# A fused attention and GLU block: where VectorE's code operations stand against background jobs at the end of a head group

## The chip, the cores and the metric

The kernel runs on one core of a Trainium2 chip. The metric is the device time of one execution in microseconds (us). An execution that was profiled gives, beside its time, the span from its first to its last instruction and the record of every instruction in it.

## The reference

```python
x = A_x                                             # (1, 2048, 512) bf16
h  = x + attention(layernorm(x), A_wqkv, A_wo)      # 32 heads of 16
h2 = h + glu(layernorm(h), B_w_gate, B_w_up, B_w_down)   # F = 1792

# attention: scores = q k^T * 16**-0.5; p = softmax(scores); o = p v; o @ wo
# glu:       (sigmoid(x @ w_gate) * (x @ w_up)) @ w_down
```

The bulk is the softmax: 32 heads x 2048 queries x 2048 keys is 134 million exponentials.

## The kernel before, in words

**Tiling.** The scores are computed transposed, 128 keys in the partitions and 512 queries in the free dimension, for one head: such a block is a *unit*. There are 2048 units. The heads come in groups: 32 *head groups* in the order of a list `gseq`, each of 64 units (16 key tiles by four row positions j). Six groups are four heads by 512 queries, the other 26 ("wide") eight heads by 256 queries, two heads to a unit. Three units make a *score tile* (`pss`, 128x1536 in PSUM, two buffers), so there are 683 score tiles, numbered through all groups.

**Who computes the exponentials.** For each score tile ScalarE runs `exp` over three units (a 128x1536 instruction) or over two (128x1024, line 1227), and in the second case VectorE does the third unit with integer arithmetic: a first operation `J` out of PSUM (line 1054) makes the bits of an approximate power of two, and when four units of J (sometimes fewer) are together in one tile, three further additions `code` (line 1074, 128x2048 for four units) make three more bit patterns of other rounding. J and the three codes are all multiplied with V and summed, so a unit on VectorE costs one J, three quarters of a code instruction, and four products on TensorE in place of one. The three code operations that wait to be issued are a `Chain` in the list `chains`.

**What follows.** TensorE multiplies each exponential with `Vaug` (V and a column for the sums) into one accumulator `acc` (line 1028, a single PSUM bank, one group at a time). When all products of a group are in, VectorE transposes `acc` into `xs` (line 970), divides (lines 932 and 934) and turns the result into `ot` (line 946). Only then may the products of the next group begin.

**Background work.** Everything else runs beside the exponentials, in small steps through one PSUM tile `pm` with a single buffer: projections of V, K and Q, and, block by block of 256 rows, the output projection with the residual (`wo_add`, lines 695 and 708), the layer norm (statistics at line 133, the Newton steps for the inverse root in lines 657 to 680, the scaling at line 720, the transposes on TensorE at line 151 and VectorE's copy out of `pm` at line 734), the gate and up products (line 160; `th`, the tanh on ScalarE at line 759, and `hT` on VectorE at line 743) and the down products (line 753 writes `ob`). The helper `quarters` at line 160 issues most of these matmuls. `fill` (line 505) issues a matmul whose result nobody reads, where TensorE would be little used.

**What sets the order.** The program is one straight line of instructions per engine. While it is built, a planner steps through three virtual clocks, `T["P"]`, `T["A"]` and `T["D"]` for TensorE, ScalarE and VectorE, with costs written in the code; the engine whose clock is earliest takes its next step (`pe_step` at line 1131, `act_step` at 1182, `dve_step` at 1241), and that step is issued. So the order of each engine's queue is fixed in the program, and on the chip each instruction waits only for what it needs. `act_step` takes a ready ScalarE job such as `th` before the next `exp` if the job's inputs are ready by the planner's clock no later than 100 ns after that `exp` could start (line 1188), and it also decides whether VectorE gets a unit of the tile, by the backlog of VectorE. `dve_step` takes, in this order: a ready background job that fits before the next J; the next J whose scores are done; a ready background job out of `dq` (line 1257); the next operation of the first chain (line 1263). `nxt["e"]` counts the score tiles whose `exp` has been issued, `lasts[group]` is the number of the last tile of a group, and `st["cur"]` the place in `gseq` of the group whose products TensorE is at.

Of the kernel before, what the change touches and what calls it, by code (L numbers as in the profile page):

```python
# [26 lines left out]
def kernel(  # L27
# [174 lines left out]
    class Task:  # L202
        def __init__(self, name, deps, opts, bank=0, frees=0):
            self.name, self.deps, self.opts, self.bank, self.frees = name, deps, opts, bank, frees
            self.end = None
            tasks[name] = self
# [221 lines left out]
    dq, aq, chains = [], [], []  # L428
# [8 lines left out]
    st = State(**{"n": 0, "open": False, "cur": 0, "pm": None, "mark": None, "acc": None, "mode": "b", "work": "b", "ot": 0})  # L437
# [7 lines left out]
        return aq[-1]  # L445

    class Chain:
        def __init__(self, ops, after):
            self.ops, self.after = deque(ops), after

        def left(self):
            return sum(o[0] for o in self.ops)
# [8 lines left out]
    def next_chain():  # L461
        return chains[0]

    def pop_chain():
        c = next_chain()
        T["D"] += c.cost()
        _, _, f = c.ops.popleft()
        c.after.append(object())
        prior["op"] = c.after[-1]
        f()  # L470
        if not c.ops:
            chains.remove(c)
# [161 lines left out]
    gseq = [(0, 0), (1, 0), (2, 0)]  # L634
# [221 lines left out]
    firsts, lasts = {}, {}  # L856
# [52 lines left out]
    NPT = 6  # L909
    PRESS = 3  # L910
    EASY = 400
    RATE, LATE, BACK, GEND, QMAX = 0.7, 700, 2500, 2000, 24

    ring = []
# [124 lines left out]
    NCODE = len(CODE_STEP)  # L1039
# [8 lines left out]
    def dexp_first(src, un):  # L1048
        if not half:
            half.append(dvx.tile([P, NJ, QC], U16, name="J", bufs=NJB))  # L1050
            first_codes.append([1])
        J, held = half[0], first_codes[-1]
        k = len(half) - 1
        first = nc.vector.tensor_scalar(out=J[:, k, :], in0=src, scalar1=128 * SC * LOG2E,  # L1054
                                        scalar2=float(CODE_BASE), op0=ALU.mult, op1=ALU.add)
        half.append(un)
        held[0] += 1
        avq.append(Unit(un.u, J[:, k, :].bitcast(BF16), un.n, T["D"] + 680, held))
        prior["op"] = J
        if k == NJ - 1:  # L1060
            dexp_rest()
        return first

    def dexp_rest():
        J, uns = half[0], half[1:]
        half.clear()
        k = len(uns)
        j = J[:, 0:k, :]
        mine = first_codes[-1]
        mine[0] += NCODE - 1  # L1070

        def code(i):
            c = dvx.tile([P, NJ, QC], U16, name="code", bufs=CB)[:, 0:k, :]
            nc.vector.tensor_scalar(out=c, in0=j, scalar1=CODE_STEP[i], scalar2=None, op0=ALU.add)  # L1074
            mine[0] -= 1
            held = [k]
            codes.append(held)
            avq.extend(Unit(un.u, c[:, m, :].bitcast(BF16), un.n, T["D"] + 85, held)
                       for m, un in enumerate(uns))
            for un in uns:  # L1080
                due[un.u[0], un.u[1], un.u[3]] -= i == NCODE - 1
        chains.append(Chain([(75 + 134 * k, 0, lambda i=i: code(i)) for i in range(NCODE)], [J]))

    def drop_read():
        for c in (codes, first_codes):
            while c and not c[0][0]:
                c.popleft()
# [41 lines left out]
    nxt = {"s": 0, "e": 0}  # L1129
# [52 lines left out]
    def act_step():  # L1182
# [15 lines left out]
        if half and not jq and left_in.get(half[-1].u[:2], 0) < CLOSE:  # L1198
            dexp_rest()
# [7 lines left out]
        if (len(tl) == GU and not 10 <= n < 20 and len(jq) < 2  # L1207
# [9 lines left out]
            if good:  # L1217
                pick = good[0]
            elif can and back <= EASY:
                pick = can[0]  # L1220
# [20 lines left out]
    def dve_step():  # L1241
        t = T["D"]
        job = next((j for j in dq if j.ready() is not None and j.ready() <= t), None)
        if job and jq and t - sc_end[jq[0][0]] < 400:
            dq.remove(job)
            job.place("D")
            return
        drop_read()
        if jq and sc_end[jq[0][0]] + LAT <= t + WAITJ and (half or len(first_codes) < NJB):
            n, pss, un, ex = jq.popleft()  # L1250
            first = dexp_first(pss, un)
            T["D"] = max(t, sc_end[n] + LAT) + 600
            ex_end[n] = max(un.end, T["D"])
            tc.declare_no_dep(first.ins, ex.ins, reason="other banks of the tile")
            readers[n] = (ex, first)
            return
        for job in dq:
            r = job.ready()
            if r is not None and r <= t + 60:
                dq.remove(job)  # L1260
                job.place("D")
                return
        if chains:
            pop_chain()
            return
        T["D"] = t + 40
# [21 lines left out]
    while nxt["e"] < N or jq:  # L1288
        e = nxt["e"]
        if e == N:  # L1290
            dve_step()
            continue
        steps[min("PAD", key=lambda k: T[k])]()
        if nxt["e"] > e:
            after_exp(e)
    if half:
        dexp_rest()
# [106 lines left out]
```

## Time and profile before

| | |
|---|---|
| time, median of 3 runs | 826.86 us (826.76 to 828.12) |
| profiled execution, its time | 826.86 us |
| profiled execution, its span | 825.1 us |
| ScalarE busy | 779.8 us (95%) |
| TensorE matmuls busy | 751.6 us (91%) |
| VectorE busy | 734.3 us (89%) |
| `exp` on ScalarE, line 1227 | 683 instructions, 727.8 us |
| `J` on VectorE, line 1054 | 478 instructions, 318.1 us |
| `code` on VectorE, line 1074 | 387 instructions, 237.4 us |
| `acc` products, line 1028 | 6337 instructions |
| `hT`, line 743, out of `pm` | 49 instructions, 33.3 us |
| `th`, line 759, out of `pm` | 49 instructions, 30.7 us |

How to read it: a row of the profile gives the line, the engine, the operation, output and inputs by the program's names, the form, and the count; then the time in which the engine was busy with these instructions, the mean length of one in ns, and the engine's idle time just before them, with what ended most of that idle time. Instructions of one engine can overlap a little, so the busy time may be below count times mean. What lies outside the span, 826.86 - 825.1 = 1.8 us, belongs to no instruction.

### The profile page before, as it was taken

Reading aid. Unit: us, or ns where it says so; the run is one execution under the profiler, and the core shown is the slowest. Engines: PE = TensorE matmul, PEld = TensorE weight load, DVE = VectorE, ACT = ScalarE, POOL = GpSimd, SP = SyncE. Lnnn points to the kernel's source line nnn. Section 1 sums busy time; section 2 is a strip of 40 time slices with the busy share of each in tenths; the row PEclk is TensorE's granted clock in tenths of the full one; section 3 lists DMA queues with packets and bytes.
Section 4 is the critical chain, followed back from the end, with each engine's and each line's share of the span. In section 5 each row is a group of like instructions: output and inputs, shape, how many; then the busy total and the mean of one; then the engine's idle time right before and its main releaser. Section 6 shows DMA issues by size and latency. Waiting matters only on the chain.

```text
span 825.1 us, 34604 instructions
## 1 busy us (share of the span) xinstructions
PE 751.6 (91%) x15255; PEld 364.5 (44%) x15259; DVE 734.3 (89%) x1415; ACT 779.8 (95%) x804; POOL 3.2 (0%) x8
## 2 busy tenths in 40 slices
PE   4889988887889999999999999999899999999988
PEld 2322223333335344555444444553455455455546
DVE  8849999997999999999989899889999889899972
ACT  6899999998999999999989999999999999989972
POOL 1000000000000000000000000000000000000000
PEclk9999999999999999999999999999999999999999
DMA  9700011015001121122022211220132022134110
GB/s 259 130 2 4 16 34 27 13 31 159 8 16 54 42 82 35 47 82 78 16 74 61 64 36 47 81 78 16 45 104 84 28 80 79 48 98 141 43 39 16
DMA packets 90717, 49.47 MB, mean 60 GB/s; under 512 B 20820, under 2 KB 90120, under 8 KB 90568
## 3 DMA queue, kind: packets, MB, share of 16 engines
q1 hardware_dynamic: 88936, 46.15, 21.1%
q8 instruction: 121, 1.98, 0.9%
q10 hardware_dynamic: 1632, 1.11, 0.4%
q14 instruction: 28, 0.23, 0.1%
HBM read 37.62 MB, written 2.10 MB: 48 GB/s over the span
## 4 chain that ended last, share of the span: by engine, by line
ACT 45%; PE 33%; issue 14%; DVE 7%; DMA 0%; ACTq 0%; DVEq 0%
ACT pt L1227 42%; PE pm L160 11%; PE pss L887 9%; PE acc L1028 9%; DVE J L1054 2%; ACT th L759 2%; PE gu L155 2%; DVE code L1074 1%; PE hp L1369 1%; DVE xs L970 1%; PE b L151 0%; DVE st L133 0%; DMA code<-in_A_x_dram 0%; DVE hT L743 0%; DVE xn L238 0%
## 5 line engine op out<-in xcount | busy, mean ns | idle before, releaser
L1227 ACT ACTIVATE pt<-pss 128x1024 bf16<-128x1024 f32 (+1 forms) x683 | 727.8, 1192 | 9.4 <-PE pss L887 6.6
L1054 DVE TENSOR_SCALAR J<-pss 128x512 uint16<-128x512 f32 x478 | 318.1, 681 | 24.5 <-PE pss L887 22.9
L887 PE MATMUL pss<-QT,KT 32*128 32x256 bf16 (+1 forms) x3712 | 269.5, 284 | 50.4 <-ACT pt L1227 39.6
L1074 DVE TENSOR_SCALAR code<-J 128x2048 uint16<-128x2048 uint16 (+3 forms) x387 | 237.4, 643 | 0.3
L1028 PE MATMUL acc<-pt,Vaug 128*17 128x256 bf16 (+1 forms) x2837 | 219.2, 286 | 2.0 <-ACT pt L1227 0.8
L887 PEld LDWEIGHTS <-KT 32*128 32x128 bf16 x3712 | 84.9, 92 | 251.3 <-ACT pt L1227 128.8
L1028 PE MATMUL acc<-code,Vaug 128*17 128x256 bf16 (+1 forms) x2625 | 186.4, 284 | 0.0
L1028 PEld LDWEIGHTS <-Vaug 128*17 128x17 bf16 x6337 | 139.7, 90 | 97.8 <-issue 82.2
L1028 PE MATMUL acc<-J,Vaug 128*17 128x256 bf16 (+1 forms) x875 | 137.2, 284 | 0.1
L160 PE MATMUL pm<-xnT,wgu 128*32 128x256 bf16 x3136 | 117.6, 275 | 1.6 <-DVE hT L743 0.8
L160 PEld LDWEIGHTS <-wgu 128*32 128x32 bf16 x3136 | 77.6, 96 | 27.2 <-issue 23.5
L160 PE MATMUL pm<-wd,hT 128*32 128x512 bf16 x784 | 56.1, 382 | 0.0
L743 DVE SCALAR_TENSOR_TENSOR hT<-th,pm 128x512 bf16<-128x512 f32 x49 | 33.3, 679 | 10.1 <-PE pm L160 8.8
L759 ACT ACTIVATE th<-pm 128x512 f32<-128x512 f32 x49 | 30.7, 626 | 8.3 <-PE pm L160 7.3
L970 DVE STREAM_TRANSPOSE xs<-acc 128x512 f32<-128x512 f32 x32 | 22.8, 712 | 11.5 <-PE acc L1028 11.3
L160 PEld LDWEIGHTS <-hT 128*32 128x32 bf16 x784 | 16.0, 95 | 19.6 <-issue 13.1
L160 PE MATMUL pm<-xnT,wq_sb 128*32 128x512 bf16 x256 | 20.5, 391 | 0.2 <-DVE kr L566 0.2
L160 PE MATMUL pm<-xnT,wk_sb 128*32 128x512 bf16 x256 | 19.7, 383 | 0.1
L151 PE MATMUL b<-ident_bf,xn 128*128 128x128 bf16 x64 | 6.5, 265 | 12.1 <-DVE xn L238 11.4
L160 PE MATMUL pm<-wo_sb,ot 128*32 128x512 bf16 x224 | 17.2, 382 | 0.1
L946 DVE STREAM_TRANSPOSE ot<-o 128x256 bf16<-128x256 bf16 x32 | 13.6, 433 | 0.1
L604 DVE TENSOR_SCALAR sh<-pm,kcol 8x512 bf16<-8x512 f32 x16 | 11.8, 735 | 1.9 <-PE pm L600 1.7
(126 smaller groups left out, 327.2 us busy)
## 6 DMA issues: line engine op xcount, KB each, us to landing
wgu<-in_B_w_gate_dram SPq DMA_DIRECT2D x49, 256.0 KB
wgu<-in_B_w_up_dram SPq DMA_DIRECT2D x49, 256.0 KB
KT<-ones SPq DMA_DIRECT2D x7, 512.0 KB
out_dram<-ob SPq DMA_DIRECT2D x16, 128.0 KB
QT<-qd SPq DMA_DIRECT2D x116, 16.0 KB
KT<-kd SPq DMA_DIRECT2D x28, 64.0 KB
wd<-in_B_w_down_dram SPq DMA_DIRECT2D x1, 1792.0 KB
xr<-in_A_x_dram SPq DMA_DIRECT2D x14, 128.0 KB
```

The source lines that it names most:

```text
L155: nc.tensor.matmul(ps, lhsT=lhsT, rhs=rhs, start=start, stop=stop)
L160: nc.tensor.matmul(ps[r, :], lhsT=lhsT[:, r], rhs=rhs, start=start, stop=stop, tile_position=(0, 32 * j), skip_group_check=True)
L604: nc.vector.tensor_scalar(out=sh[:], in0=ps2[0:8, :], scalar1=-0.505, scalar2=kcol[p][:, 0:1], op0=ALU.mult, op1=ALU.add)
L743: nc.vector.scalar_tensor_tensor(out=hT[:, 2 * k:2 * k + 2, :].rearrange("p f q -> p (f q)"), in0=th[:], scalar=1.0, in1=ps, op0=ALU.add, ...
L759: nc.scalar.activation(out=th[:], in_=ps, func=ACT.Tanh, scale=0.5)
L887: mm = nc.tensor.matmul(pss[:, ui, a * w:(a + 1) * w], lhsT=KT[hg[a]][32 * j:32 * j + 32, kt * P:(kt + 1) * P], rhs=(QT0[q] if g == 0 and ...
L946: nc.vector.transpose(out=ot[:], in_=o2[:, i * NB:(i + 1) * NB, :] .rearrange("p b r -> p (b r)"))
L970: j = st["acc"] = dve(630, lambda: nc.vector.transpose(out=xs[:].rearrange("p b r -> p (b r)"), in_=acc[:]), Mark(T["P"]))
L1028: nc.tensor.matmul(acc[32 * j:32 * j + VW, a * w:(a + 1) * w], lhsT=Vaug[:, kt, 4 * hg[a] + j, :], rhs=un.ap[:, a * w:(a + 1) * w], start= ...
L1054: first = nc.vector.tensor_scalar(out=J[:, k, :], in0=src, scalar1=128 * SC * LOG2E, scalar2=float(CODE_BASE), op0=ALU.mult, op1=ALU.add)
L1074: nc.vector.tensor_scalar(out=c, in0=j, scalar1=CODE_STEP[i], scalar2=None, op0=ALU.add)
L1227: ex = nc.scalar.activation(out=pt[:, lo:lo + wa, :], in_=pss[:, lo:lo + wa, :], func=ACT.Exp, scale=SC)
```

## The change

A chain now carries the group that its units belong to. In `dve_step`, behind the J and ahead of the background jobs, a new step is tried: if the first chain belongs to the group that TensorE's products are at, and the `exp` of that group's last score tile has been issued, the next code operation of that chain goes first. `HURRY` is 0: "has been issued" is meant exactly.

```diff
     class Chain:
-        def __init__(self, ops, after):
-            self.ops, self.after = deque(ops), after
+        def __init__(self, ops, after, group):
+            self.ops, self.after, self.group = deque(ops), after, group
...
+    HURRY = 0
...
-        chains.append(Chain([(75 + 134 * k, 0, lambda i=i: code(i)) for i in range(NCODE)], [J]))
+        chains.append(Chain([(75 + 134 * k, 0, lambda i=i: code(i)) for i in range(NCODE)], [J], uns[0].u[:2]))
...
             readers[n] = (ex, first)
             return
+        if chains and chains[0].group == gseq[st["cur"]] and lasts[chains[0].group] < nxt["e"] + HURRY:
+            pop_chain()
+            return
         for job in dq:
             r = job.ready()
             if r is not None and r <= t + 60:
```

Because the planner issues what its clocks bring next, an operation that changes place moves all later choices with it: which tiles give a unit to VectorE, where background steps of TensorE fall, and where `th` stands among the `exp`.

## The prediction, made before the changed kernel was run

> **What bounds the kernel now.** I read the page's first part, then the busy time of the stretch from the first to the last `exp`, then ScalarE's waits in that stretch. The columns of the second fence are the stretch, its length, and the busy time of TensorE, of its weight loads, of VectorE, ScalarE and GpSimd; then the granted clock and the DMA columns.
>
> ```profile
> PE 751.6 (91%) x15255; PEld 364.5 (44%) x15259; DVE 734.3 (89%) x1415; ACT 779.8 (95%) x804; POOL 3.2 (0%) x8
> ```
>
> ```profile
> 33.00:795.70 762.70, 707.41 (x14918) 337.24 (x14918) 695.85 (x1306) 746.36 (x732) 0.30 (x1) 1.00 0.19 54
> ```
>
> ```profile
> ACT th L759 <- PE pm L160: 7.3, 5, 3.0
> ACT pt L1227 <- PE pss L887: 6.6, 14, 1.9
> ACT pt L1227 <- PE acc L1028: 0.9, 1, 0.9
> ```
>
> In the stretch of 762.7 us ScalarE is busy for 746.36, idle for 16.3; TensorE has 55 us to spare and VectorE 67. So the stretch lasts as long as ScalarE's work plus its waits, and the last fence names 14.8 us of those. What the change is worth is what it does to these two sums.
>
> Where the 14.8 us lie I took from ScalarE's timeline: three of the waits, 1.49 us before 251.05, 2.99 before 418.27 and 2.40 before 733.05, together 6.9, are a `th` at the first gate product of a new block. Each lies within 2.5 us after a transpose of `acc` (249.3, 415.9, 731.8), so at a group's end; all waits so placed make 9.0. The last of the three, ScalarE, VectorE and TensorE in order of time:
>
> ```profile
> 729.62 1.03 ACT L1227 ACTIVATE pt<-pss 128x1024 bf16<-128x1024 f32 x1
> ...
> 729.92 0.41 DVE L734 COPY xnT<-pm 128x512 bf16<-128x512 bf16 x1
> 730.25 1.02 DVE L1074 TENSOR_SCALAR code<-J 128x1024 uint16<-128x1024 uint16 x2
> 730.71 0.40 PE L887 MATMUL pss<-QT,KT 32*128 32x256 bf16 x6 [0.52 <-DVE code L1074]
> ...
> 731.04 0.40 PE L151 MATMUL pm<-ident_bf,xnT 128*128 128x128 bf16 x4
> ...
> 731.47 0.43 DVE L734 COPY xnT<-pm 128x512 bf16<-128x512 bf16 x1 [0.20 <-PE pm L151]
> 731.81 0.71 DVE L970 STREAM_TRANSPOSE xs<-acc 128x512 f32<-128x512 f32 x1
> 731.95 1.06 PE L160 MATMUL pm<-xnT,wgu 128*32 128x256 bf16 x32 [0.20 <-DVE xnT L734]
> ...
> 733.05 0.60 ACT L759 ACTIVATE th<-pm 128x512 f32<-128x512 f32 x1 [2.40 <-PE pm L160]
> ```
>
> The reader is to see a string with nothing beside it: the `exp` ends at 730.65, releases a score bank, TensorE does scores, the last layer-norm transposes, VectorE copies them, TensorE does the gate product, and only then `th` runs. Scores for a next `exp` lay ready from about 731.1, but `th` stands ahead of it in ScalarE's queue.
>
> **The change, part by part.** I compared the instruction orders of the two built kernels by engine, and noted at each choice of the planner what the new step passed.
>
> *Choices.* The new step is taken 18 times, and 9 times it passes a ready job, at the ends of 5 of the 32 groups: once a maximum of K (line 566), once a layer-norm statistic (line 133), seven times a Newton step (three different ones, the one up to three times). In the old order 19 jobs in 6 groups go ahead of such codes: the K maximum, one Q shift, one seed and four steps of Newton, six scalings at line 720, three copies at line 734, three `hT`. Fifteen of the 19 stand at exactly the three group ends above.
>
> *ScalarE's work.* The planner now gives VectorE 474 units instead of 478: 475 `exp` of 128x1024 instead of 479, and 208 of 128x1536 instead of 204. Rows by form give 1065 and 1491 ns, so 4 x 0.426 = +1.7 us on the engine that bounds. No cover: it counts in full.
>
> *ScalarE's waits.* In TensorE's old order, three of the 49 gate products come behind two score tiles more than ScalarE has `exp` ahead of the `th`, so that both score banks are filled first and the second of these tiles has to wait for the `exp` just before `th`. These are the three strings above (the `th` behind 198, 347 and 625 `exp`). In the new order none of the 49 is so placed: the codes close `acc` ahead of the layer-norm chain, the blocks begin later (behind 208, 352 and 631 `exp`), and each gate product stands with one or no score tile in excess. So the 6.9 us should go. Bounds: nothing goes if the same string forms elsewhere (0); all waits at group ends go (9.0). I take 6.9 less 0.2, since the other 29 ends keep 9.0 - 6.9 = 2.1 us, 0.07 each: -6.7.
>
> *VectorE's work.* Four J at 681 ns less, -2.7; codes of four, three, two and one units go 327 to 333, 27 to 15, 12 to 15, 21 to 15: 6 x 682 - 12 x 549 + 3 x 417 - 6 x 286 = -3.0. Hidden behind ScalarE, 0; were VectorE the bound, it would be -5.7.
>
> *TensorE's work.* 6337 products become 6307; the chain shows 32 in 0.98 us, so -0.9. Fill matmuls (line 505) go from 19 to 23 at 383 ns, +1.5, in gaps. Within the 55 us to spare: 0.
>
> *The passed jobs.* A job is late by one to three codes, 0.7 to 2.0 us at 682 ns. What is queued behind: the scalings and transposes of the block, so its first gate product. ScalarE takes `exp` meanwhile, which covers it. If that cover went, the lateness would reach the end: the last `th` out of `pm` moves from behind 658 to behind 660 of 683 `exp`, two of about 1.0 us, and 23 remain to hide the down products; 0. The K maximum issues four small DMAs on SyncE's queue, ahead of which other loads may now stand; the only wait on them was 0.2 us (line 572): 0. The number of DMAs is unchanged, and GpSimd's queue is not passed.
>
> *Sum.* +1.7 - 6.7 = -5.0 us on the profiled 825.1 span and 1.8 around it, 826.86, which is also the median of the runs: 821.9, say 822.
>
> **The clock.** The granted clock (the third column from the right) fell in two places of the stretch. The first:
>
> ```profile
> 184.50:189.40 4.90, 3.58 (x58) 1.40 (x53) 2.86 (x6) 2.78 (x4) 0.00 (x0) 0.66 0.09 22
> ```
>
> ScalarE lost 4.90 - 2.78 = 2.1 us there. The other dip (0.78 over 412 to 417 us) surrounds the second of the three strings, behind TensorE gaps of 0.2 to 0.6 us.
> [...]
>
> **The rivals.**
> (1) *The stall moves.* Each block still begins with a serial chain, Newton, scaling, transpose, copy, gate. If `th` is late again, or the `exp` behind TensorE's catching-up, 3.5 to 6.9 us stay and 1.7 are added: 826.86 + 1.7 - 3.4 to - 0 gives 825.2 to 828.6. For it: at group ends the planner's costs and the chip part company, as its own `th` placed 3 us early show. Against: no gate product has the old position.
> (2) *TensorE runs dry* (the other side). The passed jobs hold the only `pm` tile, so background stops while `acc` waits for the codes; dips follow at the ends where jobs are passed. Price: 1.7 + 2.1 a dip, with the stalls replaced by equal ones: one dip 830.7, two 832.8. It decides from the point where more than 5.0 us of new waits appear. For it: four more fills mean that the planner itself sees TensorE idle. Against: 9 passes only, of 0.7 us each, and both engines have over 55 us to spare.
> (3) *More is won.* Closing `acc` earlier also clears the waits of scores at other ends: all 9.0 and half of the remaining 14.8 - 9.0 = 5.8: 826.86 + 1.7 - 11.9 = 816.7. Against: only 5 ends have a pass, and one wait (1.89) is at the start of the stretch.
> (4) *The step does nothing.* The orders exclude this: 18 uses, and other queues from the third group on.
>
> **How the numbers follow.** Forecast (3.5 to 9.0 us of waits saved, 819.6 to 825.1) 0.50; rival 1 0.20; rival 2 0.17; rival 3 0.13. A re-planned order also shifts small waits everywhere, which nothing in the trace prices; that is why the forecast holds no more. Measured to 0.2%, or 1.65 us, "the same" is 825.2 to 828.5: 0.15 of rival 1 and little else. Faster is 0.50 + 0.13 = 0.63, slower 0.17 + 0.05 of rival 1 = 0.22. The range leaves out one tenth on each side: 816.5, the foot of rival 3, to 831.0, just past one dip.
>
> **What would show it.** Right: ScalarE's waits for `pm` at `th` down from 7.3 to under 1.5 us; 208 long `exp`; ScalarE's idle time between first and last `exp` near 10 us against 16.3. Wrong: the `th` sum stays, or waits of `exp` for scores grow from 6.6 by as much as was saved (rival 1); more stages with a clock under 0.8, and fill matmuls amid idle TensorE (rival 2). The forecast itself falls if the removed stalls were no loss, because ScalarE's later `exp` would have waited for TensorE anyway.

## The result, and the profile after

The changed kernel takes 823.89 us (823.04 to 824.68), the kernel before 826.86: ratio 0.9956, 95% interval 0.9945 to 0.9967. It is faster by 3.0 us, where 4.9 was forecast; the time lies in the range. The profiled execution has a span of 822.1 us.

The page's busy line; then the stretch from the first to the last `exp` (columns as in the prediction: stretch, its length, busy time of TensorE, weight loads, VectorE, ScalarE, GpSimd, granted clock, DMA); then ScalarE's waits in that stretch:

```profile
PE 750.8 (91%) x15229; PEld 363.0 (44%) x15233; DVE 728.3 (89%) x1402; ACT 782.6 (95%) x804; POOL 3.2 (0%) x8
```

```profile
33.00:792.73 759.73, 706.43 (x14892) 335.64 (x14892) 689.98 (x1293) 749.09 (x732) 0.30 (x1) 1.00 0.20 54
```

```profile
ACT pt L1228 <- PE pss L887: 5.8, 13, 1.9
ACT pt L1228 <- PE acc L1029: 1.8, 1, 1.8
ACT th L759 <- PE pm L160: 0.2, 1, 0.2
```

The stretch is 3.0 us shorter (762.7 to 759.7), and the work after the last `exp` takes the same 29.4 us. Inside it ScalarE is busy 2.7 us longer and idle 5.7 us less (16.3 to 10.6). The three long waits of `th` are gone, 7.3 us to 0.2. One wait is new, in the middle line: an `exp` that waits for an accumulator product. The groups of `exp` by form (line, engine, operation, form, count, busy time, mean length, idle time before):

```profile
L1228 ACT ACTIVATE pt<-pss 128x1024 bf16<-128x1024 f32 x475 | 464.4, 1065 | 7.3 <-PE pss L887 5.2
L1228 ACT ACTIVATE pt<-pss 128x1536 bf16<-128x1536 f32 x208 | 297.6, 1493 | 3.6 <-PE acc L1029 1.8 <-PE pss L887 0.6
```

Four units moved to ScalarE, as the order said. The new wait, with what stood ahead of it on VectorE:

```profile
409.79 5.58 ACT L1228 ACTIVATE pt<-pss 128x1536 bf16<-128x1536 f32 x5
...
412.80 0.40 PE L1029 MATMUL acc<-code,Vaug 128*17 128x256 bf16 x8
...
413.21 0.69 DVE L753 SCALAR_TENSOR_TENSOR ob<-pm,h 128x512 bf16<-128x512 f32 x1
413.82 0.68 DVE L1055 TENSOR_SCALAR J<-pss 128x512 uint16<-128x512 f32 x1
...
414.42 1.00 DVE L720 TENSOR_SCALAR xnT<-h,mv,rstd 128x512 bf16<-128x512 f32 x2
...
415.33 0.71 DVE L971 STREAM_TRANSPOSE xs<-acc 128x512 f32<-128x512 f32 x1
...
416.67 0.28 PE L1029 MATMUL acc<-pt,Vaug 128*17 128x256 bf16 x1
...
417.12 0.24 DVE L933 RECIPROCAL rec<-xs 128x16 f32<-128x16 f32 x1
...
417.16 2.37 ACT L1228 ACTIVATE pt<-pss 128x1536 bf16<-128x1536 f32 x2 [1.79 <-PE acc L1029]
```

The last product of group 15 ended at 413.2. The transpose that empties `acc` came 2.1 us later, behind `ob`, a J and two scalings in VectorE's queue; only then could products of the next group run and give `pt` buffers back. They start at 416.7, before the division does (417.1): of the work at a group's end the transpose alone holds them back, not the division or `ot`.

### The profile page after: what moved, and what is told of

It is laid out like the page before. It is cut to its first block, busy times and chain, and to the rows that moved or that the text cites. A ratio compares the mean times of both kernels' runs of the same rounds, so it can differ in the third digit from the quotient of the medians.

```text
span 822.1 us, 34525 instructions
## 1 busy us (share of the span) xinstructions
PE 750.8 (91%) x15229; PEld 363.0 (44%) x15233; DVE 728.3 (89%) x1402; ACT 782.6 (95%) x804; POOL 3.2 (0%) x8
## 4 chain that ended last, share of the span: by engine, by line
ACT 46%; PE 34%; issue 13%; DVE 6%; DMA 0%; ACTq 0%; DVEq 0%
ACT pt L1228 44%; PE pm L160 12%; PE acc L1029 10%; PE pss L887 10%; ACT th L759 2%; DVE J L1055 2%; PE gu L155 2%; PE hp L1373 1%; DVE xs L971 1%; PE b L151 0%; DVE st L133 0%; DMA code<-in_A_x_dram 0%; DVE xn L238 0%; DVE hT L743 0%; DVE kmin L297 0%
## 5 line engine op out<-in xcount | busy, mean ns | idle before, releaser
L1055 DVE TENSOR_SCALAR J<-pss 128x512 uint16<-128x512 f32 x474 | 314.8, 681 | 21.0 <-PE pss L887 19.6
L1029 PE MATMUL acc<-code,Vaug 128*17 128x256 bf16 (+1 forms) x2595 | 182.0, 284 | 0.0
L160 PE MATMUL pm<-xnT,wgu 128*32 128x256 bf16 x3136 | 114.6, 274 | 1.7 <-DVE hT L743 1.2
L160 PEld LDWEIGHTS <-wgu 128*32 128x32 bf16 x3136 | 75.8, 96 | 28.4 <-issue 24.8
L155 PE MATMUL gu<-xnT,KT 128*128 128x256 bf16 x112 | 12.4, 273 | 0.7 <-ACT xnT L1356 0.7
```

The lines of the kernel that those rows point to most:

```text
L155: nc.tensor.matmul(ps, lhsT=lhsT, rhs=rhs, start=start, stop=stop)
L160: nc.tensor.matmul(ps[r, :], lhsT=lhsT[:, r], rhs=rhs, start=start, stop=stop, tile_position=(0, 32 * j), skip_group_check=True)
L1029: nc.tensor.matmul(acc[32 * j:32 * j + VW, a * w:(a + 1) * w], lhsT=Vaug[:, kt, 4 * hg[a] + j, :], rhs=un.ap[:, a * w:(a + 1) * w], start= ...
```

## The experiments

Two theories. **Q** is the prediction's: at the three stalls `th` stands ahead of an `exp` whose scores lie ready, so the order of ScalarE's queue loses the time. **P** grew out of the first experiment: ScalarE stops there because the group's accumulator is emptied too late, and what the rule does is to empty it sooner. The *close* below is the time from the end of a group's last `exp` to the start of the transpose of `acc`, read off the timelines. Of the other ends of the kernel before, end 25 closes in 5.6 us, and its wait of 0.9 us for a product is there; the rest take 4.2 us or less.

Repeated runs of one program differ with the granted clock. In the trace of the kernel before it is 0.50 in two windows of 3.41 us, from 186.11 and from 414.80 us, and 1.00 in the 3.41 us on either side of each. In 208 runs of the kernels here, against each kernel's own mean, the time rises by 1.17 us for each window of 3.4 us at half clock (their number worked out as lost clock times span over 1.7 us), and that accounts for 84% of the scatter. So each row has its mean number of windows, and the mean time brought to none by that slope (standard error 0.1 to 0.3 us, 0.6 for e4). The five runs of the first comparison have 1.6 windows and 821.9 us at none.

| run | median us | ratio to before (95%) | windows | us at none | close at 8, 15, 28 (us) | waits of ScalarE: `th`, `acc`, scores |
|---|---|---|---|---|---|---|
| before (84 runs) | 828.0 to 828.2 | 1 | 2.8 | 824.7 | 6.1, 6.1, 7.9 | 7.3, 0.9, 6.6 |
| e1 | 831.09 | 1.0040 (1.0026 to 1.0054) | 2.7 | 827.6 | 6.1, 5.7, 8.1 | 0.4, 8.1, 7.1 |
| e2 | 827.44 | 0.9992 (0.9980 to 1.0003) | 2.4 | 824.2 | 6.1, 5.7, 3.1 | 3.4, 0.9, 7.3 |
| e3 | 828.55 | 1.0006 (0.9990 to 1.0023) | 3.2 | 824.8 | 2.2, 6.0, 7.9 | 3.2, 4.5, 8.4 |
| e4 | 833.82 | 1.0075 (1.0053 to 1.0098) | 6.5 | 826.1 | 1.3, 3.3, 2.1 | 0.3, 0, 12.9 |
| e5 (changed) | 824.81 | 0.9974 (0.9958 to 0.9990) | 2.6 | 822.5 | 3.6, 5.4, 3.2 | 0.2, 1.8, 6.7 |
| e6 | 826.98 | 0.9995 (0.9981 to 1.0010) | 1.9 | 825.2 | 6.1, 6.2, 7.9 | 7.3, 0, 6.5 |
| e7 | 828.29 | 1.0001 (0.9984 to 1.0019) | 2.6 | 825.4 | 6.1, 5.7, 7.9 | 3.1, 0, 10.3 |
| e8 | 828.39 | 1.0006 (0.9994 to 1.0017) | 3.9 | 823.7 | 3.6, 5.4, 3.2 | 0.2, 0.4, 11.4 |
| e9 | 823.57 | 0.9949 (0.9934 to 0.9963) | 2.1 | 821.3 | 3.6, 3.7, 2.9 | 0, 0, 7.4 |
| e10 | 826.86 | 0.9993 (0.9979 to 1.0007) | 1.8 | 825.1 | 6.1, 6.9, 6.5 | 1.7, 3.4, 7.2 |
| e11 | 829.83 | 1.0019 (0.9998 to 1.0040) | 6.5 | 822.3 | 1.8, 2.5, 3.1 | 0.8, 1.6, 11.9 |
| e12 | 824.03 | 0.9951 (0.9938 to 0.9964) | 2.6 | 821.0 | 3.9, 3.1, 2.8 | 0, 0.4, 9.0 |

**e1: the three `th` one `exp` later, all other queues untouched.**

```diff
+            st["th"] = st.get("th", 0) + 1
+            if st["th"] in (1, 15, 43):
+                late_th.append(job.fn)
+                job.fn = lambda: None
             job.place("A")
...
+        while late_th:
+            late_th.pop()()
         T["A"] = start + 51 + 427 * wa
```

> The kernel before, with one thing moved: the first tanh of the three blocks that stalled is issued on ScalarE one exp later; every other queue is as before. Theory Q (the loss is ScalarE's queue: a tanh stands ahead of an exp whose scores lie ready): an exp of 904 ns fits into each of the waits of 1.49, 2.99 and 2.40 us, so 3 x 0.9 = 2.7 us are saved, about 824.2 us, and ScalarE's waits of tanh for pm fall from 7.3 to about 4.5. Theory S (the string on TensorE and VectorE is what takes the time; whatever ScalarE has in its queue waits as long): 826.9 us, the same waits under another name.

Q missed, and S is right about the waits but not about the time: it became 3 us slower. In its trace the waits of `th` are nearly gone and three waits of an `exp` for an accumulator product are there in their place, of 1.75, 1.80 and 3.71 us (the 32 gate products of the block took 1.90 us ahead of the last, 1.06 in the kernel before). ScalarE's waits, then the third place, where the `th` follows the `exp`:

```profile
ACT pt L1231 <- PE acc L1028: 8.1, 4, 3.7
ACT pt L1231 <- PE pss L887: 7.1, 17, 1.9
ACT th L759 <- PE pm L160: 0.4, 2, 0.2
```

```profile
731.72 0.72 DVE L970 STREAM_TRANSPOSE xs<-acc 128x512 f32<-128x512 f32 x1
...
734.08 1.02 ACT L1231 ACTIVATE pt<-pss 128x1024 bf16<-128x1024 f32 x1 [3.71 <-PE acc L1028]
...
735.00 0.59 ACT L759 ACTIVATE th<-pm 128x512 f32<-128x512 f32 x1
```

In the kernel before, ScalarE's timeline at the same place, from the end of group 28 to the stall:

```profile
723.82 3.32 ACT L1227 ACTIVATE pt<-pss 128x1024 bf16<-128x1024 f32 x3
727.37 3.28 ACT L1227 ACTIVATE pt<-pss 128x1536 bf16<-128x1536 f32 x3 [0.23 <-PE pss L887]
```

Six `exp` of the next group, and `pt` has six buffers. None can be given back before a product of that group, and none of these may run before `acc` is emptied. So when ScalarE came to the `th`, the `exp` behind it could not have run either. Theory Q falls: the scores lay ready, the buffer did not. `th` was only the first instruction to show the wait. The planner shows the same: `act_step` also takes a ready job when the next `exp` may not run at all because the oldest of the six `pt` is still unread (lines 1186 and 1188), and of the 49 `th` exactly these three are placed so, with the scores of the next tile already issued. In the changed kernel none is. And behind each late `th` the next `exp` waits another 0.62 us for scores, 1.9 us in all, against the 2.9 that e1 lost at no windows.

**e2: the rule at group end 28 alone**, so that the order is as before up to about 600 us.

```diff
-        if chains and chains[0].group == gseq[st["cur"]] and lasts[chains[0].group] < nxt["e"] + HURRY:
+        if st["cur"] == 28 and chains and chains[0].group == gseq[st["cur"]] and lasts[chains[0].group] < nxt["e"] + HURRY:
```

> The changed kernel with the new rule at one group end alone, number 28 of 0 to 31, so that all is as before until about 600 us. Three units go back to ScalarE, +1.3 us. Theory Q: the stall of 2.40 us at 733 goes, the tanh sum falls from 7.3 to 4.9: 826.9 + 1.3 - 2.4 = 825.8 us, and ScalarE's idle time before 600 us is unchanged. Rival (the gain of the change is spread over all group ends by an earlier close of acc): the end of group 28 gives 1/32 of it, and 1.3 are added: 828 us.

The close at 28 fell from 7.9 to 3.1 us and the stall of 2.40 us went. The median difference is 0.6 us and 0.5 at no windows, with 1.3 us of `exp` added: the direction expected, at half of the expected size (1.1 us), and the interval includes 1.

**e3: no rule, another order.**

```diff
-    LS = 1.1
+    LS = 1.09
```

> The kernel before without the rule, but with the planner's factor LS at 1.09 in place of 1.1: the order shifts, and by the instruction orders the first two of the three stalled tanh no longer stand ahead (one is left). One unit fewer on ScalarE's side is moved, -0.4 us. Theory Q (what counts is how many tanh stand so): 1.49 + 2.99 are saved, 826.9 - 4.5 - 0.4 = 822.0 us, tanh sum near 2.5. Rival (codes ahead of jobs is what gains): no gain, 826.5 to 827.

A miss for Q: only one `th` stands as before, and there is no gain. The closes of 15 and 28 stayed at 6.0 and 7.9 us, and ScalarE's waits for `th` and for products are together 3.2 + 4.5 = 7.7 us, against 8.2 before. Where the `th` stands changes the wait's name. End 8 did close sooner, in 2.2 us, but the new order closed ends 2 and 3 in 4.9 and 4.5 us, and an `exp` waited 0.86 and 1.14 us for a product there; so a close can stop ScalarE below 5 us too.

**e4: the transpose of `acc` ahead of every other VectorE operation**, on the changed kernel.

```diff
     def dve_step():
         t = T["D"]
+        job = st["acc"]
+        if job is not None and job.end is None and job in dq and job.ready() is not None and job.ready() <= t + 60:
+            dq.remove(job)
+            job.place("D")
+            return
```

> The changed kernel, and the transpose that empties acc goes ahead of every other VectorE operation as soon as its products are in. The new wait of 1.79 us of an exp for an accumulator product, at 417 us, comes from that transpose standing behind an ob, a J and two scalings; if so it goes, and with 207 long exp in place of 208 (-0.4) the time is 823.9 - 1.8 - 0.4 = 821.7 us. Rival (the passed jobs are late in turn and new waits replace it): 823.9 or more.

It does what it should, the closes are short and no `exp` waits for a product, but it loses 6 us to before. ScalarE's waits for scores doubled to 12.9 us, and the clock lost 6.5 windows a run, 3.7 more than before; by the slope those are 4.3 of the 6 us. Closing sooner is not worth any price.

**e5: the changed kernel again**, with more runs beside the kernel before.

> The changed kernel as it is, beside the kernel before on one chip and with many runs, to lay each run's time over its mean granted clock: the runs of the kernel before in the experiments so far lie on a line of about 1.1 us for each half-clock window of 3.4 us, 2.9 windows a run in the mean. Theory P (the change is worth its earlier close of the accumulator): at an equal number of windows it is 2 to 4 us below the kernel before, and the windows are as many. Rival (the change is worth fewer windows): the two lie on one line.

With as many windows it is 2.2 us below: the gain is not luck with the clock. In the first comparison, with 1.6 windows, it is 2.8 us below by the same reckoning, so a part of the 3.0 us there may be the clock.

**e6, e7, e8: a seventh `pt` buffer**, on the kernel before, on e1 and on the changed kernel, the order of every queue unchanged. To make room, `qd`, `sq` and `ob` have one buffer in place of two; the last two `ob` use the two of `xr`.

```diff
-    ptp = ctx.enter_context(tc.tile_pool(name="ptp", bufs=6))
+    ptp = ctx.enter_context(tc.tile_pool(name="ptp", bufs=7))
...
-        qd = work.tile([P, QC], BF16, name="qd", bufs=2)
-        sq = work.tile([P, QC], BF16, name="sq", bufs=2)
+        qd = work.tile([P, QC], BF16, name="qd", bufs=1)
+        sq = work.tile([P, QC], BF16, name="sq", bufs=1)
```

> The kernel before with the same order of instructions on every engine and a seventh buffer for the exponentials pt (to make room, qd, sq and ob have one buffer in place of two). Theory P (at the end of a group ScalarE stops because all pt buffers hold exponentials that wait for the accumulator): the one wait of an exp for an accumulator product goes, 0.9 us; the three tanh still stand ahead of the next exp and still wait, about 7 us. So about 1 us less than before. Theory Q (queue order alone): no change at all. Rival (narrower qd, sq, ob cost): more than before.

> The kernel with the three tanh one exp later, and the seventh pt buffer. With six buffers this exp waited for an accumulator product in all three places (1.75, 1.80 and 3.71 us) and the kernel was 3 us slower. Theory P: with a buffer free the exp runs at once, the three waits for accumulator products go, and an exp of 0.9 us is won in each of the three places: 5 to 6 us below the same kernel with six buffers, 2 to 3.5 below the kernel before. Rival (the exp would wait for scores just as long): no better than with six.

> The changed kernel, order unchanged, with the seventh pt buffer. Theory P: its one wait of an exp for an accumulator product (1.8 us at group end 15) goes: 1.5 to 2 us below the changed kernel. Rival: that time is lost to the next wait behind it: no change.

The waits for products vanish in e6 and e7 (0.9 and 8.1 us to 0) and nearly in e8 (1.8 to 0.4): the buffer was what those `exp` waited for. e6 is no faster for it (825.2 us at no windows against 824.7, where 1 us less was expected). e7 is 2.2 us below e1 at no windows, less than half of what was expected, and no better than before: the `exp` ran, and then `th` still waited 0.6, 0.6 and 1.5 us, and the `exp` behind it 0.6 each for scores. Beside e6, which has the same buffers and the `th` where they were, it is no better either (825.4 against 825.2 us): even where the `exp` can run, moving the `th` behind it wins nothing. e8 missed: its waits for scores rose from 6.7 to 11.4 us, with more windows. What of that is due to the narrower `qd`, `sq` and `ob` was not separated. More buffers move the stop; they don't shorten the string.

**e9, e10: the rule at the ends 8, 15, 28 alone, and at all others alone.**

```diff
+        if st["cur"] in (8, 15, 28) and chains and ...        # e9
+        if st["cur"] not in (8, 15, 28) and chains and ...    # e10
```

> The changed kernel with the rule at the group ends 8, 15 and 28 alone, where the three long waits were. Theory P (what pays is that the accumulator of these groups is emptied sooner): from the last exp of the group to the transpose of acc 6.1, 6.1 and 7.9 us fall below 5, the gain is that of the whole change: ratio to before about 0.997, waits of tanh for pm under 1.5 us. ScalarE gets five units more than before (+2.1 us). Rival (all ends pay a little): a tenth of the gain, and the 2.1 us make it slower than before, 1.002.

> The changed kernel with the rule at all group ends but 8, 15 and 28. Theory P: the ends 8, 15 and 28 close as late as in the kernel before (about 6 us or more), the waits of ScalarE for a tanh or for an accumulator product there remain, about 6 to 8 us together, four units more on ScalarE add 1.7: not faster than before, ratio 1.000 to 1.003. Rival (the new order as such is luckier, wherever the rule acts): 0.996 to 0.998.

Both came out as P had it. At the three ends alone the rule gives the whole gain (0.9949), at all the others none that the runs show (0.9993). ScalarE's waits in e9, then in e10:

```profile
ACT pt L1228 <- PE pss L887: 7.4, 17, 1.9
```

```profile
ACT pt L1228 <- PE pss L887: 7.2, 15, 1.9
ACT pt L1228 <- PE acc L1029: 3.4, 2, 2.1
ACT th L759 <- PE pm L160: 1.7, 2, 1.5
```

In e9 no wait is left but that for scores; in e10, with closes of 6 to 7 us, 5.1 us of the others stay, though only one `th` stands there as it did. A part of e9 is the new order and not the rule: end 25, where the rule does not act in e9, closes in under 4 us there, and its wait of 0.9 us is gone. Whether e9 is better than the changed kernel is open: the two intervals to before overlap.

**e11: one score tile sooner.**

```diff
-    HURRY = 0
+    HURRY = 1
```

> The changed kernel with HURRY = 1: the codes go first from one score tile before the group's last exp is issued. Theory P: the group ends close at most as late as in the changed kernel, the one wait of 1.8 us at end 15 goes, two units more on ScalarE add 0.9: ratio to before 0.996 to 0.997, as the changed kernel or a little under it. Rival (jobs passed over more often leave TensorE without work): more half-clock windows than 2.6 a run and more waits of exp for scores than 6 us: 1.000 or more.

The rival's numbers came out. At no windows it would equal the changed kernel (822.3 against 822.5), but it has 6.5 windows a run. Four of those in its trace, worked out from the clock lost, lie in the 15.0 us from 246.0; the columns are those of the stretch above, the granted clock, 0.54, the third number from the right:

```profile
246.00:261.00 15.00, 13.62 (x160) 4.96 (x163) 9.46 (x22) 10.70 (x10) 0.00 (x0) 0.54 0.00 1
```

ScalarE lost 15.0 - 10.7 = 4.3 us in them.

**e12: more fill.**

```diff
-    FILL = 1600.0
+    FILL = 2000.0
```

> The changed kernel with FILL at 2000 in place of 1600, so 42 matmuls that nobody reads in place of 23, meant to hold the clock. The changed kernel had 2.6 half-clock windows of 1.2 us each in a run. Theory W (windows come where TensorE is little used for 3.4 us): half of them go, 1.5 us are won, two units more on ScalarE cost 0.9, so 0.5 to 1 us below the changed kernel, ratio to before 0.996. Rival (fill stands in the way of scores): windows fall but waits of exp for scores grow, the time is that of the changed kernel or above.

There are 42 fills in place of 23, and 2.6 windows as with 23. That does not refute theory W: whether any of the added fills stood just ahead of a place where a window came was not shown. The time is that of the changed kernel within the intervals; the order differs in more than the fills, so what gain it may have is not theirs.

## Why the prediction was right, and where it was not

**The bound.** Right: the stretch is ScalarE's work plus its waits, and both sums moved as far as the time did.

**ScalarE's work, +1.7.** Right: 475 and 208 `exp`, means 1065 and 1493 ns. Beside it the busy time grew by another 1.0 us that was not forecast.

**ScalarE's waits, -6.7.** The size of the `th` waits was right, -7.1. That it came out was partly luck, since the cause was wrong. The step that failed is that "`th` stands ahead of it in ScalarE's queue", as if the next `exp` could have run from 731.1. In e1 it could not; it waited for a `pt` buffer. What moved the `th` also closed `acc` sooner. All three signs that the prediction had named for being right came true (`th` waits 0.2 us, 208 long `exp`, 10.6 us idle), and none of them tells the queue from the buffer. In place of that step the runs put this: at the ends 8, 15 and 28 the close took 6 to 8 us, about six `exp`, because background jobs went ahead of the group's codes (of the 15 that the prediction counts there, 13 are layer-norm jobs and two are the `ob` of line 753, one of them at 727.9 us in the trace; what the prediction calls three `hT` are three such `ob`); the rule brings it to 3.6, 5.4 and 3.2. e9 and e10 show no gain from the rule at any other end.

**The terms that were missing, +2.0 us together.** With the cause mistaken, `th` in a new place seemed enough, and all else at the ends was set to 0.07 us each. But 5.4 us at end 15 is still at the edge, and 1.79 us of the stall stayed there as a wait for a product, against one of 0.9 us before, at end 25, which now closes in under 4 us: +0.9. That is rival 1 in a single place. Waits for scores fell by 0.8, not the 2.9 of rival 3, and those of `th` by 0.4 more than forecast. ScalarE's idle time fell by only 5.7 while its named waits fell by 7.0, so 1.3 us came back as gaps too short for the list of waits, and 1.0 us as the longer busy time: 0.9 - 0.8 - 0.4 + 1.3 + 1.0 = 2.0, the way from -5.0 to -3.0. That ScalarE, with its stalls gone, runs closer behind TensorE and meets it in small pieces would explain the last two; no run isolates it.

**VectorE, TensorE, passed jobs: 0.** No run contradicts it for nine passes. e11 speaks against it for a rule that acts sooner: its waits for scores rose to 11.9 us and its windows to 6.5 a run.

**Rival 2, TensorE dry and the clock.** Not in the change (2.6 windows a run, 2.8 before), but windows are what sank e11 and most of what sank e4, at 6.5. The price forecast for a window, 2.1 us, was too high: 1.17 by the slope, 1.1 each for the four of e11. The clock changes of a trace lie on one grid of 3.41 us: in the kernel before they stand at 186.11, 189.53, 414.80 and 418.22 us, 1, 66 and 1 steps apart, in the changed kernel at 114.95, 118.36, 203.70 and 207.11, 1, 25 and 1 steps apart. How many windows are at half clock differs between runs of one program: 1.0 to 4.9 in the kernel before.

## What to carry to other kernels

A wait shows only the first instruction that meets it (the 7.3 us under `th` stood as 8.1 us under `acc` in e1): before an instruction is blamed for standing ahead of another, ask what else the other would have waited for, and count the buffers. Where groups share one accumulator, look at the time from the last producer to the emptying of it, and compare it with what the ring of buffers holds; a priority for the last producers is worth most at the few ends where it exceeds that. And a change of order is to be judged with the clock windows counted, since they alone scatter the runs of the kernel before by about 4.6 us (1.0 to 4.9 windows).

## What was not expected of the hardware

Between the first and the last `exp` the traces of the kernel before and of the changed kernel have two half-clock windows each, and each of the four lasts 3.41 us. In e11 the granted clock was 0.54 over 15.0 us, which makes 13.8 us at half clock, while TensorE counted as busy for 13.62 of the 15. A busy share says less there: in the two of the kernel before the matmuls were busy for 96 and 100% of the time, but the six score products of a tile took 0.61 us at 186.25, inside the first, and 0.40 at 183.99, ahead of it at full clock. One run of a kernel lost the clock of none to ten windows (none in a run of e10, ten in one of e11).

What stood ahead of a half-clock window can be read off the grid of these two traces. Between 33 and 790 us they have 437 windows of 3.41 us at full clock. Four of them stand right ahead of a half-clock one, and in these the matmuls were busy for 1.91 us (from 182.70) and 2.40 (from 411.39) in the kernel before, for 2.24 (from 111.54) and 1.81 (from 200.28) in the changed kernel, so none of the four was idle. In seven of the other 433 they were busy for no more than 2.40 us either, in one for 2.15 (from 56.92, the changed kernel), and no half-clock window followed. Why four of these eleven were followed and seven were not, and what ends a row of windows, stays open.
